# Transposing the second batch's keys and queries with the DMA crossbar instead of TensorE, in memory lent by weights that are not yet loaded

## The chip, the cores and the metric

The kernel runs on one core of a Trainium2 chip. The metric is device time in microseconds (us) of one execution. Times below are medians. A span given by a profile is 1 to 2 us shorter than the time of an execution.

## The reference, cut to what matters

```python
# 4 batches, 8 heads, 768 tokens, 64 dimensions, 16 clusters per head
q_assign = argmax(einsum('bhsd,hcd->bhsc', q_n, c_n)); k_assign = ...      # fp32 decides the cluster
mask   = q_assign[:, :, :, None] == k_assign[:, :, None, :]
attn   = softmax(where(mask, q @ k.T / 8, -1e9)) @ v
x      = attn as (3072, 512)
out    = sum over 4 experts e of p[:, e] * (relu(x @ w1[e]) @ w2[e])       # 512 -> 1024 -> 512
```

Every key and query is needed transposed (dimension on the partitions), in fp32 for the cluster scores and in bf16 for attention.

## The kernel before

TensorE works through attention steps and expert matmuls woven together. A generator per batch ("preparation") is paced beside them: so many of its steps between two attention steps. For batch 1 it transposes on TensorE. Batches 2 and 3 already go over the DMA crossbar (the transposing path of the DMA engines), which the program gives 16-bit elements: each fp32 tensor is **split** by GpSimd into low and high halves, the halves are **crossed** (transposed) by DMA, and GpSimd **merges** them again.

```python
class Assign:
    def turn(self, y, copy, shared=False):          # one head, three 128x128 fp32 transposes on TensorE
        ...
        nc.tensor.matmul(tp[:, c0:c0 + 128], raw[...][:, ...], ident, is_transpose=True)
        ...
        copy(t32, tp[:, :m * w])                    # PSUM to SBUF, VectorE in batch 1
    def cast(self, y, r, copy): ...                 # fp32 to the bf16 rows of KF or QF, GpSimd in batch 1
    def scores(self, copy): ...                     # four fp32 matmuls (TensorE), one copy
    def back(self): ...  # transposes the scores;  top(): marks the best cluster with a one-hot row (VectorE)
    def send(self, j, r):                           # one-hots to 16 rows of KF or QF
        (nc.gpsimd if self.b or ... else nc.sync).dma_start(...)

class Crossed(Assign):
    def split(self, n): ...                         # pool(h16[...], raw[...][:, z::2]), 768 halves a partition
    def cross(self, j): ...                         # nc.sync.dma_start(out=t16, in_=h16, transpose=True)
    def merge(self, n): ...                         # pool(all[...][:, z::2], t16[...])
    def casts(self): ...                            # two VectorE casts of 64x1536

def load_w(e):                                      # 2 x 2 MB fp32 from HBM, cast to bf16 by the DMA
    nc.gpsimd.dma_start(out=W1[e], in_=...)
    nc.gpsimd.dma_start(out=W2[e], in_=...)

for y, x in enumerate(xs):                          # keys 0-3, queries 0-3, keys 4-7, queries 4-7
    if b == 1:                                      # preparation of batch 1, 31 steps
        t = 12 * (y // 2) + 4 * z
        for j in range(HG):
            put(t + j, lambda x=x, j=j: turn(x, j)) # turn on TensorE, two casts on GpSimd
        ...
        put(at, lambda x=x: x.scores(dve))
        put(at + 1 + z, x.back, x.top, x.scale_onehot, x.cross_onehot)
        put(at + 4 + z, x.send_all)
...
put(1 + 18 * g, lambda g=g: load_w(2 + g))          # experts 2 and 3
```

Each engine has one queue, which in all traces here it works off in program order; SyncE's queue issues the crossings, GpSimd's the weight loads and the sends.

The softmax here doesn't subtract the row's maximum and nothing guards it: scores larger than these inputs give would overflow.

## Time and profile before

| | before |
|---|---|
| time, median of 4 runs | 475.19 us (475.13 to 475.93) |
| TensorE busy | 98% of the span |
| VectorE, ScalarE, GpSimd busy | 48%, 58%, 39% |
| granted TensorE clock | 1.000 |
| first matmul of expert 2 / of expert 3 | 85.28 us / 101.32 us |

The last row gives two landmarks: TensorE's first 128x128 matmul group of expert 2 and of expert 3. All preparation of batch 1 that concerns us lies before the second. The lines of the page are shown in the prediction.

### The profile page before, as it was taken

How to read it: one execution, taken by the hardware profiler on the slowest of the kernel's cores; microseconds unless marked ns; L12 is line 12 of the kernel's file. 1: busy time of each engine (PE TensorE's matmuls, PEld its weight loads, DVE VectorE, ACT ScalarE, POOL GpSimd, SP SyncE). 2: the span in 40 equal slices, each digit the busy share in tenths (PEclk: the TensorE clock that was granted, in tenths of full speed). 3: DMA queues.
4: the chain of work that ended last, by engine and by line, in shares of the span. 5: the costliest groups of instructions: out<-in, count | busy, mean ns of one | idle time of the engine just before them, and what ended most of it. 6: DMA issues, size and time to landing. Idle time of an engine off the chain costs nothing.

```text
span 474.3 us, 11380 instructions
## 1 busy us (share of the span) xinstructions
PE 466.8 (98%) x4529; PEld 331.6 (70%) x4529; DVE 226.0 (48%) x558; ACT 277.1 (58%) x502; POOL 186.1 (39%) x301
## 2 busy tenths in 40 slices
PE   8999999999999999999999999999999999999997
PEld 4778777776776767677676767776766766667665
DVE  5964764321316664321234544423878767675112
ACT  5757655445665656566565655665665675664442
POOL 5936469180653694450442933000332132220000
PEclk9999999999999999999999999999999999999999
DMA  8999962927664940603657545202100100100101
GB/s 278 259 211 344 241 128 42 177 44 174 96 122 114 199 118 18 159 15 62 150 141 123 115 114 160 68 16 73 50 13 8 54 10 8 36 28 12 44 2 44
DMA packets 75981, 48.27 MB, mean 102 GB/s; under 512 B 51544, under 2 KB 70680, under 8 KB 75928
## 3 DMA queue, kind: packets, MB, share of 16 engines
q1 hardware_dynamic: 66680, 38.22, 32.7%
q0 software_dynamic: 8576, 9.25, 11.0%
q8 instruction: 35, 0.57, 0.6%
q10 hardware_dynamic: 672, 0.08, 0.1%
q14 instruction: 18, 0.15, 0.1%
HBM read 37.31 MB, written 6.30 MB: 92 GB/s over the span
## 4 chain that ended last, share of the span: by engine, by line
PE 94%; DVE 2%; DMA 2%; SPq 0%; issue 0%; ACT 0%; ACTq 0%
PE ps_mo L724 35%; PE ps_mo L743 35%; PE ps_s L634 9%; PE ps_av L661 7%; PE ps_s L547 1%; DMA raw<-in_q_dram 1%; DMA kf<-oht 1%; PE ps_misc L242 1%; PE ps_misc L547 1%; PE ps_misc L400 1%; PE ps_mo L400 1%; PE ps_mo L242 1%; DVE kf L315 1%; PE ps_mo L267 0%; PE ps_misc L267 0%; DVE oh L287 0%
## 5 line engine op out<-in xcount | busy, mean ns | idle before, releaser
L640 ACT ACTIVATE at<-ps_s 128x512 bf16<-128x512 f32 x252 | 147.7, 596 | 119.0 <-PE ps_s L634 103.9
L724 PE MATMUL ps_mo<-xT,w1b 128*128 128x256 bf16 (+1 forms) x1664 | 195.8, 264 | 0.0
L743 PE MATMUL ps_mo<-w2b,hT 128*128 128x512 bf16 (+2 forms) x784 | 190.3, 375 | 0.0
L724 PEld LDWEIGHTS <-w1b 128*128 128x128 bf16 x1664 | 146.3, 98 | 25.1 <-issue 1.2
L730 ACT ACTIVATE hT<-ps_mo 128x512 bf16<-128x512 f32 x192 | 114.7, 598 | 60.7 <-PE ps_mo L724 58.0
L752 DVE SCALAR_TENSOR_TENSOR oacc<-ps_mo,psb,oacc 128x512 f32<-128x512 f32 (+1 forms) x74 | 54.3, 734 | 130.7 <-PE ps_mo L743 130.4
L743 PEld LDWEIGHTS <-hT 128*128 128x128 bf16 x784 | 67.1, 98 | 57.5 <-issue 3.1
L634 PE MATMUL ps_s<-qf,kf 80*128 80x256 bf16 (+1 forms) x456 | 82.5, 267 | 0.9 <-ACT at L640 0.4
L661 PEld LDWEIGHTS <-at 128*128 128x128 bf16 x1152 | 69.9, 97 | 15.3 <-issue 1.7
L661 PE MATMUL ps_av<-vx,at 128*128 128x65 bf16 x1152 | 80.3, 193 | 0.0
L647 POOL TENSOR_TENSOR at<-at,same 128x512 bf16<-128x512 bf16 x24 | 28.2, 1174 | 98.5 <-ACT at L640 82.8
L634 PEld LDWEIGHTS <-kf 80*128 80x128 bf16 x456 | 42.0, 98 | 20.8 <-issue 1.9
L564 DVE TENSOR_SCALAR same<-qf,late 128x256 bf16<-128x256 bf16 x144 | 39.3, 324 | 0.0
L377 POOL COPY t<-t 128x768 uint16<-128x768 uint16 x32 | 35.5, 1116 | 0.0
L647 DVE TENSOR_TENSOR at<-at,same 128x512 bf16<-128x512 bf16 x48 | 21.6, 449 | 25.7 <-ACT at L640 25.7
L358 POOL COPY h<-raw 128x768 uint16<-128x768 uint16 x16 | 13.0, 825 | 37.3 <-DMA raw<-in_q_dram 30.7
L668 DVE RECIPROCAL zr<-ps_av 128x4 f32<-128x4 f32 (+1 forms) x50 | 8.9, 178 | 33.9 <-PE ps_av L661 33.8
L361 POOL COPY h<-raw 128x768 uint16<-128x768 uint16 x16 | 13.0, 826 | 28.9 <-DMA raw<-in_q_dram 20.4
L336 POOL DMA_DIRECT2D kf<-oht x32 | 15.4, 496 | 22.8 <-DMA oht<-oh 13.1
L750 DVE TENSOR_SCALAR oacc<-ps_mo,psb 128x512 f32<-128x512 f32 x18 | 13.5, 749 | 22.7 <-PE ps_mo L743 22.7
L416 POOL COPY st<-sct 128x384 uint16<-128x384 uint16 x16 | 10.6, 708 | 31.7 <-DMA sct<-scs 31.7
L336 POOL DMA_DIRECT2D qf<-oht x40 | 20.0, 509 | 6.2 <-DVE oht L313 3.9
(130 smaller groups left out, 281.5 us busy)
## 6 DMA issues: line engine op xcount, KB each, us to landing
raw<-in_v_dram SPq DMA_DIRECT2D x8, 768.0 KB, 5.7
out_dram<-oacc SPq DMA_DIRECT2D x23, 256.0 KB, 2.2
raw<-in_k_dram SPq DMA_DIRECT2D x7, 768.0 KB, 6.3
raw<-in_q_dram SPq DMA_DIRECT2D x6, 768.0 KB, 5.3
w1b<-in_moe_w_dram POOLq DMA_DIRECT2D x4, 1024.0 KB, 11.5
w2b<-in_moe_w_dram POOLq DMA_DIRECT2D x4, 1024.0 KB, 16.8
qf<-nos SPq DMA_DIRECT2D x2, 768.0 KB, 4.0
xT<-xn SPq DMA_TRANSPOSE x80, 2.4
```

The lines of the kernel that those rows point to most:

```text
L336: (nc.gpsimd if self.b or self.i0 and self.g else nc.sync).dma_start(out=self.rows(slice(D, D + CL), j, r), in_=self.oht[p0:p0 + CL, :self.w])
L377: pool(self.all[:, y * w:(y + 1) * w].bitcast(U16)[:, z::2], self.t16[:, (2 * z + y) * w:(2 * z + y + 1) * w])
L564: nc.vector.tensor_scalar(same[:, x * 256:(x + 1) * 256], clusters(b)[:, g, w, k // 2, k % 2, :], key_nos[b % 2][:, g, 8 * i + 4 * (k // 2 ...
L634: nc.tensor.matmul(sp[:, x * n:(x + 1) * n], KF[b % 2][:K, h, r, i * 128:(i + 1) * 128], QF[b % 2][:K, h, rs[0]:rs[-1] + 1, w * 128:(w + 1 ...
L640: nc.scalar.activation(at, sp, ACT.Exp, scale=scale)
L647: (nc.gpsimd if n4 in POOL_STEPS else nc.vector).tensor_tensor(at, at, same_cluster(b, w, cur), op=ALU.mult)
L661: nc.tensor.matmul(av[:, h % 2, m, :], at[:, c0:c0 + 128], VX[b % 2][:, h, 2 * i + r, :], start=(first and x == 0 and m == 0), stop=(last ...
L724: nc.tensor.matmul(ph[:, x * n:(x + 1) * n], W1[e][:, i, (f + x) * 128:(f + x + 1) * 128], xT[:, i, :], start=(i == 0), stop=(i == ND - 1))
L730: nc.scalar.activation(ht, ph, ACT.Relu)
L743: nc.tensor.matmul(po, hT[f // per][:, c0:c0 + 128], W2[e][:, f, c], start=(f == 0), stop=(f == NF - 1))
L750: nc.vector.tensor_scalar_mul(oacc, po, pap)
L752: nc.vector.scalar_tensor_tensor(oacc[:, c], po, pap, oacc[:, c], op0=ALU.mult, op1=ALU.add)
```

## The change

The intent is to take 48 fp32 transposes off the engine that bounds the kernel, TensorE, and with them their copies out of PSUM (TensorE's output memory) off VectorE. Memory for the halves is short; the change puts those of the first two tensors into the weight buffers of experts 2 and 3, so those weights can be loaded only later. The core of the diff:

```diff
+        def lent(self, w):
+            return w[self.borrows].rearrange("p i c -> p (i c)").bitcast(U16)[:, :2 * HG * QW]
...
+        if b == 1:
+            xs[0].borrows, xs[1].borrows = 2, 3
             for y, x in enumerate(xs):
+                g, z = divmod(y, 2)
+                t, late_cross = 16 * g + 4 * z, 3 * (y == 3)
                 for j in range(HG):
-                    put(t + j, lambda x=x, j=j: turn(x, j))
+                    put(t + j, lambda x=x, j=j: x.split(j))
+                    put(t + 1 + j + late_cross, lambda x=x, j=j: x.cross(j))
+                    put(t + 8 + j + (late_cross > 0), lambda x=x, j=j: x.merge(j))
+                put(t + 12 + (late_cross > 0), x.take_all, x.casts)
+                put(16 * g + 18, lambda x=x: x.scores(dve))
+                put(16 * g + 19 + z, x.back, x.top, x.scale_onehot, x.cross_onehot)
+                put(16 * g + 23 + z, x.send_all)
+            put(0, lambda: load_raw(upto=11))
+            put(13, lambda: load_w(2))
+            put(25, lambda: cast_v(b, 0), lambda: load_w(3))
+            put(28, lambda: load_raw(2, upto=13))
+            put(36, lambda: cast_v(b, 1))
...
-    XSTEPS = [0, 31, 63, 63]
+    XSTEPS = [0, 41, 63, 63]
```

More of the change, by code (lines that the diff above doesn't have):

```diff
@@ L344, with take_all @@
     class Crossed(Assign):
+        borrows = None
         def halves(self, x):
             return x.rearrange("p j c -> p (j c)").bitcast(U16)
+        def lent(self, w):
+            return w[self.borrows].rearrange("p i c -> p (i c)").bitcast(U16)[:, :2 * HG * QW]
+        def take_all(self):
+            self.t32s = [self.all[:, j * QW:(j + 1) * QW] for j in range(HG)]
         def split(self, n):
@@ L353, in split @@
             if n == 0:
-                self.h16 = self.halves(raws.tile([128, HG, QW], F32, name="h16", tag="raw"))
+                self.h16 = (self.lent(W1) if self.borrows is not None else
+                            self.halves(raws.tile([128, HG, QW], F32, name="h16", tag="raw")))
             dst = self.h16.rearrange("p (s y a j d) -> p s y a j d", s=2, a=A, j=2, d=D)
@@ L365, in cross @@
             if j == 0:
-                self.t16 = self.halves(raws.tile([128, HG, QW], F32, name="t16", tag="raw"))
+                self.t16 = (self.lent(W2) if self.borrows is not None else
+                            self.halves(raws.tile([128, HG, QW], F32, name="t16", tag="raw")))
             c = slice(j * 2 * QW, (j + 1) * 2 * QW)
@@ L466, in put @@
             todo.setdefault(at, []).extend(fs)
-        def turn(x, j):
-            x.turn(j, dve)
-            for r in range(2):
-                x.cast(j, r, pool)
-        for y, x in enumerate(xs):
-            z = y % 2
-            if b == 1:
-                t = 12 * (y // 2) + 4 * z
-                for j in range(HG):
-                    put(t + j, lambda x=x, j=j: turn(x, j))
-                put(t + 3, lambda: load_raw(upto=13))
-                at = 12 * (y // 2) + 8
-            else:
-                t = 8 * y
+        if b == 1:
+            xs[0].borrows, xs[1].borrows = 2, 3
+            for y, x in enumerate(xs):
+                g, z = divmod(y, 2)
+                t, late_cross = 16 * g + 4 * z, 3 * (y == 3)
@@ L483, in assigns @@
                 for j in range(HG):
                     put(t + j, lambda x=x, j=j: x.split(j))
-                    put(t + 2 + j, lambda x=x, j=j: x.cross(j))
-                    put(t + 9 + j, lambda x=x, j=j: x.merge(j))
-                put(t + 6, load_raw)
-                put(t + 15 + 4 * z, x.casts)
-                at = 16 * (y // 2) + 24
-            if b == 1:
-                put(at, lambda x=x: x.scores(dve))
-                put(at + 1 + z, x.back, x.top, x.scale_onehot, x.cross_onehot)
-                put(at + 4 + z, x.send_all)
-                continue
+                    put(t + 1 + j + late_cross, lambda x=x, j=j: x.cross(j))
@@ L495, in assigns @@
+            put(36, lambda: cast_v(b, 1))
+        for y, x in enumerate(xs if b > 1 else ()):
+            z = y % 2
+            t = 8 * y
+            for j in range(HG):
+                put(t + j, lambda x=x, j=j: x.split(j))
+                put(t + 2 + j, lambda x=x, j=j: x.cross(j))
+                put(t + 9 + j, lambda x=x, j=j: x.merge(j))
+            put(t + 6, load_raw)
+            put(t + 15 + 4 * z, x.casts)
+            at = 16 * (y // 2) + 24
             put(at, lambda x=x, t=("mo", "misc")[z]: x.scores_split(t))
@@ L504, in assigns @@
             put(at + 14 + 6 * z, x.spread_numbers)
-        for g in range(2):
-            if b == 1:
-                put(1 + 18 * g, lambda g=g: load_w(2 + g))
-                put(26 + 3 * g, lambda g=g: cast_v(b, g), lambda: load_raw(upto=13))
-            else:
-                for j in range(HG):
-                    put(36 + 8 * g + j, lambda g=g, j=j: cast_v(b, g, (j,)))
-                put(40 + 8 * g, load_raw)
+        for g in range(2 if b > 1 else 0):
+            for j in range(HG):
+                put(36 + 8 * g + j, lambda g=g, j=j: cast_v(b, g, (j,)))
+            put(40 + 8 * g, load_raw)
         for at in range(XSTEPS[b]):
@@ L893 @@
         gens.append(Paced(assigns(b), XSTEPS[b], PER_B * (b - 1) if b > 1 else S1 + 7,
-                          PER_B * b - (2 if b > 1 else -2)))
+                          PER_B * b - (2 if b > 1 else -6)))
     def woven(works, upto):
```

## The prediction

> **What bounds the kernel now.** I read the page's busy table first, then the chain that ended last, cut to the stretch in which the second batch is prepared, then the engines in order of time there. All times are microseconds.
>
> ```profile
> PE 466.8 (98%) x4529; PEld 331.6 (70%) x4529; DVE 226.0 (48%) x558; ACT 277.1 (58%) x502; POOL 186.1 (39%) x301
> PE   8999999999999999999999999999999999999997
> POOL 5936469180653694450442933000332132220000
> PEclk9999999999999999999999999999999999999999
> ```
>
> TensorE is busy from end to end at full clock: work taken from its queue shortens the program one for one, and any wait put into its in-order queue lengthens it one for one. GpSimd is at 39% on average, but slices 4 to 8 (35 to 95 us) hold 4, 6, 9, 1, 8: its room lies in waits, and this is where the change puts its work.
>
> The change concerns the 16 groups of three fp32 transposes of batch 1, found in the chain (start, duration, what) from 41.5 to 67.2. Samples:
>
> ```profile
> 41.54 0.36 PE ps_misc L242 x3
> ...
> 46.24 0.36 PE ps_misc L242 x3
> ...
> 59.76 0.49 PE ps_misc L242 x3
> ...
> 66.88 0.36 PE ps_mo L242 x3
> ```
>
> The eight groups of heads 0 to 3 sum to 2.9 us on the chain, the eight of heads 4 to 7 to 3.0: **5.9 us**, 1.2% of the program. (The 273 ns median of one such matmul is pipelined latency, not what it costs the chain, which is 0.12.)
>
> The cost of what replaces them is seen where batches 2 and 3 already go that way, in the groups by form:
>
> ```profile
> L377 POOL COPY t<-t 128x768 uint16<-128x768 uint16 x32 | 35.5, 1116 | 0.0
> L361 POOL COPY h<-raw 128x768 uint16<-128x768 uint16 x16 | 13.0, 826 | 28.9 <-DMA raw<-in_q_dram 20.4 <-DMA raw<-in_k_dram 8.4
> L336 POOL DMA_DIRECT2D kf<-oht x32 | 15.4, 496 | 22.8 <-DMA oht<-oh 13.1 <-DMA w2b<-in_moe_w_dram 5.5 <-DMA w1b<-in_moe_w_dram 4.2
> L258 POOL CAST kf<-t 64x384 bf16<-64x384 f32 x30 | 15.3, 511 | 4.1 <-ACT t L252 1.6 <-DVE t L252 1.4
> L387 DVE CAST kf<-t 64x1536 bf16<-64x1536 f32 x4 | 4.5, 1118 | 1.6 <-POOL t L377 1.6
> ```
>
> Each row has busy time, mean ns of one, idle before. Back to back on GpSimd a split starts every 0.77 (102.33 to 105.46 for four) and an undisturbed split-merge pair takes 1.73, so a merge 0.96.
>
> GpSimd's order of time around the last weights (start, duration):
>
> ```profile
> 79.57 0.81 POOL L153 DMA_DIRECT2D w1b<-in_moe_w_dram  x1
> 80.38 0.92 POOL L154 DMA_DIRECT2D w2b<-in_moe_w_dram  x1
> 81.26 2.95 POOL L336 DMA_DIRECT2D kf<-oht  x6
> 88.40 0.49 POOL L336 DMA_DIRECT2D kf<-oht  x1 [4.19 <-DMA w1b<-in_moe_w_dram]
> 94.35 0.49 POOL L336 DMA_DIRECT2D kf<-oht  x1 [5.47 <-DMA w2b<-in_moe_w_dram]
> ```
>
> After the two weight loads six sends go out, the seventh waits for the first load to land, the eighth for the second: here no more than eight transfers of this queue are outstanding. Before the change that costs nothing, since only batch 1's attention, steps later, needs what GpSimd makes.
>
> **What the Trainium skill says.** "VectorE: DVE Perf Modes", section The three transpose paths, gives 390 ns for a 128x128 bf16 transpose on TensorE (into PSUM) and 1309 ns on the crossbar (into SBUF). The crossbar is the slower way to the result but leaves TensorE free; here one transfer of six blocks lands in a median 2.8 us and occupies the SyncE queue 1.25. "DMA: Bandwidth & Descriptors", section DMA Transpose (X-bar), allows 2-byte types only: hence the halves, and the splits and merges. The same page, section SWDGE vs HWDGE vs iDMA, says that the queues of GpSimd and SyncE feed different internal queues of the same DMA engines, served in turn. The trace agrees that they share: a crossbar transfer of xT lands in a median 2.4, but in 5.4 while weights load (80 to 95). "SBUF — State Buffer", in its first section, says that one of VectorE and GpSimd blocks while the other holds the shared port pair, for instance in a fast VectorE cast. The trace agrees: the merge at 150.60 took 1.77 instead of 1.04 beside the two L387 casts at 149.01.
>
> **The change part by part.**
> Removed: 48 transposes on TensorE, -5.9 on the chain; 16 evacuations on VectorE (16 x 0.555 = 8.9) and 32 casts on GpSimd (32 x 0.51 = 16.4), both beside other work.
> Added: on GpSimd 16 splits (16 x 0.77 = 12.3) and 16 merges (16 x 0.96 = 15.4), net +11.3; on VectorE 8 casts of 64x1536 (8 x 1.1 = 8.8), net nothing; 16 crossbar transfers on SyncE (16 x 1.25 = 20 of queue time), a queue with room.
> Moved: the load of expert 2's weights from preparation step 1 to 13, expert 3's to 25; heads 0 to 3's scores from 8 to 18, the others' from 20 to 34. The generator's 41 steps run from attention step 35 to 78 (31 to 74 before).
>
> The dependency is what matters. Before, TensorE made the transposes itself and GpSimd's casts were a side product. After, TensorE's scores and VectorE's casts need GpSimd's merges, so GpSimd's in-order queue enters the chain. I lay both queues side by side.
>
> GpSimd comes free at 42.1 (its sends of batch 0 end). To the last merge that the second scores need it must do: 16 splits 12.3, 16 merges 15.4, two weight loads 2 x 1.73, 16 sends (two groups of 3.8) 7.6, four V casts 1.8: 40.6 in all. Thus **82.7 at the earliest**, without one wait.
>
> TensorE without waits: preparation step 34 is attention step 35 + 34 x 43/41 = 70.7, just after expert 2 begins at step 70. In the trace expert 2 begins at 85.3, and the steps after it take 2.7 each, so step 70.7 is at 87. Less 5.9 removed, less 2.1 for the second group's scores and turns that now come later: **79**. So even a GpSimd that never waits is 3.7 late.
>
> It will wait. (a) Heads 0 to 3: the raw queries land near 46.8 (issue 33.6, landing 13.2), so the second four splits end near 50, eight merges with the weight issue between them (1.7) near 59.4. TensorE reaches the first scores at about 56.4 and the second tensor's at 57.2: some 2.2 of wait, and VectorE then does the casts (2.2) before it copies the scores, which costs about 1.3 more: **3.5**. (b) The first sends need the one-hots, whose crossbar transfer leaves near 64 and lands near 69.5, as it runs against the weights issued at 56 (5.4 rather than 2.8). From there: sends to 73.4, the last split 74, sends 78, two merges 80, V casts and weights 83.5, six merges 89, with 0.8 lost to VectorE's casts: near 89 to 90. TensorE, now 3.5 later, arrives at 82.5: **7** of wait.
> Sum: -5.9 + 3.5 + 7 = +4.6. If GpSimd's waits vanish, only the 3.7 and part of (a) remain: about -1.
>
> **Rivals.**
> 1. The waits are hidden and the 5.9 is gained: 469.3. For it: the page's average of GpSimd, the same method working in batches 2 and 3, and a schedule that looks tuned (late crossings for the last tensor, loads after the lent memory is read). Against it: 40.6 of work in the 36.9 between 42.1 and 79. I have taken all durations from other stretches; if the pace of the steps is 4 us off, it holds.
> 2. Weights or DMA become the bound: expert 2's weights are issued near 57, land within 16 (75.9 to 94.4 is 14 for the next), needed from 80; expert 3's issued near 83, landed near 98, needed after 100. The trace before is against this by several us; it would cost 0 to 3.
> 3. VectorE, stuck in order at the casts behind the merges, fails to empty the PSUM banks of the experts, and TensorE stops earlier than at the scores. Three banks rotate there, so I find about 9 us of slack at the second casts; if this slack is smaller, the loss grows to 10 or 12 and the time to 484 or more.
>
> **Range and chances.** The gain is bounded by 5.9, so 469 is the floor and faster by over 2% (below 465.7) has hardly a chance. The working gives 479.8. Because the pace could be off in my disfavour I shade it to 478. The low end of 470 is rival 1 nearly whole; the high end of 486 is rival 3. Over 484.7 (slower by 2%) I give 0.12.
>
> **What would show it.** L242 in the chain of batch 1 gone, with about 5.9 less TensorE time: the first step. TensorE idle in front of L267 (the scores), its releaser a GpSimd merge L377 or a VectorE copy behind it, 2 to 4 us near 57 and 4 to 10 near 80: the main claim. GpSimd at 9 in slices 4 to 8; its sends L336 waiting on oht near 65 to 70. I am wrong if TensorE's row shows no gap between 50 and 95 (then 469 to 470), or if the gaps stand at expert matmuls L724 that wait for weights (rival 2) or for VectorE (rival 3).

## The result, and the profile after

| | before | after |
|---|---|---|
| time, median of 4 runs | 475.19 us | 491.79 us (490.79 to 492.25) |
| ratio | | 1.0343 (1.0329 to 1.0358): slower |
| granted TensorE clock, mean | 1.000 | 0.983 |
| first matmul of expert 2 / 3 | 85.28 / 101.32 | 83.06 / 117.82 |

Ratios are the mean time of one kernel's runs over that of the other's in the same rounds, so they are not quite the ratio of the medians. The result is correct. The prediction of 478 with a range of 470 to 486 failed: the time lies 16.6 us above the kernel before.

The page of the kernel after (busy share in 40 slices of 12.25 us, and the granted clock in tenths):

```profile
PE 465.8 (95%) x4430; PEld 328.2 (67%) x4481; DVE 232.0 (47%) x550; ACT 277.0 (57%) x502; POOL 203.1 (41%) x301
PE   7999889489999999999999999999999999999997
POOL 5928666966245469345055365100122223121000
PEclk9999999669999999999999999999999999999999
```

TensorE's row has one hole, in the eighth slice (86 to 98 us), with low clock there and in the next. Everything from slice 10 on is as before. In TensorE's own order of time (start, duration, what, and in brackets how long it stood idle just before and for whom), the hole reads:

```profile
83.06 0.61 PE L732 MATMUL ps_mo<-xT,w1b 128*128 128x128 bf16 x8
...
88.72 1.49 PE L267 MATMUL ps_misc<-t,bdc 128*32 128x384 f32 x4 [2.51 <-POOL t L387]
94.14 1.50 PE L267 MATMUL ps_misc<-t,bdc 128*32 128x384 f32 x4 [3.92 <-POOL t L387]
96.04 1.50 PE L267 MATMUL ps_mo<-t,bdc 128*32 128x384 f32 x4 [0.41 <-POOL t L387]
99.46 1.49 PE L267 MATMUL ps_mo<-t,bdc 128*32 128x384 f32 x4 [1.93 <-POOL t L387]
...
117.82 0.61 PE L732 MATMUL ps_mo<-xT,w1b 128*128 128x128 bf16 x8
```

Here L267 computes the scores of heads 4 to 7, and its releaser is each time a GpSimd merge, L387: the releaser that the prediction named (it has the line numbers of the kernel before, where the merge is L377 and the expert matmuls are L724 and L743; after, they are L387, L732 and L751). How much is lost where follows from the landmarks. Without any wait expert 2 would begin at 85.3 - 5.9 (transposes gone) - 2.1 (scores moved behind it) = 77.3 and expert 3 at 101.3 - 5.9 = 95.4. They begin at 83.1 and 117.8. So **5.8 us are lost before expert 2 (heads 0 to 3) and 16.6 more before expert 3 (heads 4 to 7)**; 5.8 + 16.6 - 5.9 = 16.5, which is the measured loss.

TensorE's two longest waits for heads 0 to 3 look different. They are not at L267 and not for GpSimd, but for VectorE, whose cast (third line) had itself waited for merges and so held up what stood behind it:

```profile
58.35 0.29 PE L685 MATMUL ps_mo<-identb,xn 128*128 128x128 bf16 x2 [2.16 <-DVE xn L678]
66.33 0.55 PE L276 MATMUL ps_misc<-ident,scs 128*128 128x128 f32 x3 [1.80 <-DVE scs L271]
```
```profile
55.04 2.71 DVE L397 CAST kf<-t 64x1536 bf16<-64x1536 f32 x2 [2.56 <-POOL t L387]
```

Why the merges come so late is in the chain of waits, from 71 us on (start, duration, what):

```profile
71.58 6.05 DMA oht<-oh
...
78.24 3.17 POOL kf L336 x7
...
82.93 2.26 POOL qf L336 x5
...
86.67 1.99 POOL t L387 x2
88.66 1.76 POOL vx L149 x4
90.42 0.76 POOL w1b L153
91.18 0.91 POOL w2b L154
92.09 2.53 POOL t L387 x3
94.62 0.29 issue
94.91 4.50 POOL t L387 x3
```

The one-hot of heads 0 to 3 (oht) leaves only at 71.6 and needs 6 us; behind it stand sixteen sends (L336), one split, two merges, the V casts (L149), the issue of expert 3's weights (L153, L154) and six more merges, all in one queue. And the start of it, on SyncE's queue and on VectorE:

```profile
43.41 14.34 SPq L378 DMA_TRANSPOSE w2b<-w1b  x8
67.31 4.17 SPq L694 DMA_TRANSPOSE xT<-xn  x2
71.58 2.05 SPq L430 DMA_TRANSPOSE oht<-oh  x1
```
```profile
94.11 4.40 DVE L397 CAST kf<-t 64x1536 bf16<-64x1536 f32 x2 [19.11 <-POOL t L387]
99.63 4.62 DVE L397 CAST qf<-t 64x1536 bf16<-64x1536 f32 x2
```

The first eight crossings (in lent memory, hence w2b<-w1b) take 1.79 on average instead of 1.25: three of them hold the queue for 2.3 to 2.7. Two transposes of xT (the attention output on its way to the experts) then hold it for 4.2, and the one-hot, which VectorE had ready at 69.0, leaves behind them. VectorE, at a cast, waited 19.1 for the merges; its two casts then take 4.4 where such pairs took 1.9 to 2.6 in the kernel before.

### The profile page after: what moved, and what is told of

The parts are those of the page before. It is cut to its first block, busy times and chain, and to the rows that moved or that the text cites. A ratio compares the mean times of both kernels' runs of the same rounds, so it can differ in the third digit from the quotient of the medians.

```text
span 490.1 us, 11262 instructions
## 1 busy us (share of the span) xinstructions
PE 465.8 (95%) x4430; PEld 328.2 (67%) x4481; DVE 232.0 (47%) x550; ACT 277.0 (57%) x502; POOL 203.1 (41%) x301
## 4 chain that ended last, share of the span: by engine, by line
PE 83%; POOL 6%; DMA 5%; DVE 3%; issue 2%; ACT 0%; SPq 0%; POOLq 0%; ACTq 0%
PE ps_mo L732 32%; PE ps_mo L751 31%; PE ps_s L642 7%; PE ps_av L669 6%; POOL t L387 3%; DMA w2b<-w1b 2%; POOL qf L336 1%; DMA oht<-oh 1%; PE ps_s L555 1%; DMA kf<-oht 1%; POOL kf L336 1%; PE ps_misc L555 1%; PE ps_s L87 1%; PE ps_mo L410 1%; DVE qf L397 1%
## 5 line engine op out<-in xcount | busy, mean ns | idle before, releaser
L732 PE MATMUL ps_mo<-xT,w1b 128*128 128x256 bf16 (+1 forms) x1664 | 196.5, 265 | 0.7 <-ACT hT L738 0.7
L751 PE MATMUL ps_mo<-w2b,hT 128*128 128x512 bf16 (+1 forms) x733 | 187.7, 377 | 2.5 <-issue 0.2
L732 PEld LDWEIGHTS <-w1b 128*128 128x128 bf16 x1664 | 146.2, 98 | 25.6 <-issue 2.2
L751 PEld LDWEIGHTS <-hT 128*128 128x128 bf16 x784 | 66.8, 98 | 59.4 <-issue 5.5
L655 POOL TENSOR_TENSOR at<-at,same 128x512 bf16<-128x512 bf16 x24 | 28.2, 1175 | 98.5 <-ACT at L648 83.0
L387 POOL COPY t<-t 128x768 uint16<-128x768 uint16 x40 | 44.8, 1145 | 0.0
L370 POOL COPY h<-raw 128x768 uint16<-128x768 uint16 x24 | 22.2, 939 | 29.5 <-DMA raw<-in_q_dram 19.4
L367 POOL COPY h<-raw 128x768 uint16<-128x768 uint16 x16 | 13.0, 827 | 37.4 <-DMA raw<-in_q_dram 30.9
L336 POOL DMA_DIRECT2D kf<-oht x32 | 15.4, 489 | 18.8 <-DMA oht<-oh 18.8
L336 POOL DMA_DIRECT2D qf<-oht x40 | 19.7, 500 | 8.3 <-DVE oht L313 3.9
## 6 DMA issues: line engine op xcount, KB each, us to landing
w2b<-in_moe_w_dram POOLq DMA_DIRECT2D x4, 1024.0 KB, 16.5
```

Of the source, the lines that this page charges most:

```text
L336: (nc.gpsimd if self.b or self.i0 and self.g else nc.sync).dma_start(out=self.rows(slice(D, D + CL), j, r), in_=self.oht[p0:p0 + CL, :self.w])
L370: pool(self.h16[:, z * HG * QW + c:z * HG * QW + c + 2 * QW], self.halves(raw[self.b, self.t, self.g])[:, 2 * c:2 * c + 4 * QW][:, z::2])
L387: pool(self.all[:, y * w:(y + 1) * w].bitcast(U16)[:, z::2], self.t16[:, (2 * z + y) * w:(2 * z + y + 1) * w])
L655: (nc.gpsimd if n4 in POOL_STEPS else nc.vector).tensor_tensor(at, at, same_cluster(b, w, cur), op=ALU.mult)
L732: nc.tensor.matmul(ph[:, x * n:(x + 1) * n], W1[e][:, i, (f + x) * 128:(f + x + 1) * 128], xT[:, i, :], start=(i == 0), stop=(i == ND - 1))
L751: nc.tensor.matmul(po, hT[f // per][:, c0:c0 + 128], W2[e][:, f, c], start=(f == 0), stop=(f == NF - 1))
```

## The experiments

Four theories, each of which could make the second group's merges late. **1:** order of GpSimd's queue, the sends in front of merges. **2:** DMA, the weight loads beside crossings and one-hots. **3:** VectorE, whose casts wait in its queue for merges, and where casts and GpSimd's copies block each other. **4:** the clock, which stays low after the hole. All edits are against the kernel after the change unless said otherwise.

| label | edit | us | ratio to before (interval) |
|---|---|---|---|
| after | | 491.8 | 1.034 (1.033, 1.036) |
| late_sends | first sends behind all merges | 491.6 | 1.035 (1.033, 1.036) |
| late_casts | VectorE's casts behind the one-hots | 487.8 | 1.026 (1.024, 1.027) |
| warm | matmuls in TensorE's waits | 493.9 | 1.038 (1.035, 1.041) |
| no_w2 | expert 2's weights not loaded | 484.6 | 1.020 (1.017, 1.022) |
| late_sends_w3 | late_sends, expert 3's weights later | 481.5 | 1.013 (1.011, 1.016) |
| reordered | all moves, more at once | 491.6 | 1.034 (1.033, 1.036) |
| g0_only | heads 0 to 3 alone | 480.4 | 1.011 (1.010, 1.013) |
| keys_only | keys alone, early weights | 503.3 | 1.059 (1.055, 1.064) |
| three_moves | late_sends_w3 and late_casts | 481.6 | 1.013 (1.010, 1.016) |
| g0_ordered | heads 0 to 3, reordered | 483.5 | 1.017 (1.015, 1.018) |
| g0_w2late | the same, expert 2's weights later | 483.2 | 1.016 (1.015, 1.018) |
| full_spaced | whole change, all findings | 477.4 | 1.004 (1.003, 1.006) |
| g0_spaced | heads 0 to 3, all findings | **473.4** | **0.996 (0.995, 0.997)** |

The kernel before measured 475.3 to 475.5 beside the runs from late_sends on. The result is correct in all of them but no_w2. The program that judges runs calls a difference under 2% "same", so all from late_sends_w3 on but reordered and keys_only count as that; the intervals say what is clear of noise.

### late_sends: only the order of the sends

```diff
-                put(16 * g + 23 + z, x.send_all)
+                put((34, 39)[g] + z, x.send_all)
```

> Only the 16 sends of the one-hots of heads 0 to 3 move on GpSimd, from preparation steps 23 and 24 to 34 and 35, behind all merges. Theory 1 (the sends, which wait 8.5 us for a one-hot and take 7.7, stand in GpSimd's queue in front of the last eight merges): those merges end near 88 instead of 99.4, TensorE's wait at the second scores falls from some 15 us to 3 to 5, and the time is 479 to 483. Theory 2 (the transfers are late because expert 2's weights are loaded beside them): the merges then wait for the crossings instead, and the time stays above 486.

Measured 491.6: nothing gained. The wait for the one-hot left GpSimd's queue as meant, and expert 3's weights were issued 10 us earlier (80.6 instead of 90.4). They fell upon the last crossings. From the chain of waits:

```profile
80.97 12.25 DMA t<-h
93.22 0.05 issue
93.28 1.99 POOL t L387 x2
```

A crossing that lands in 2.8 us undisturbed took 12.3 beside the load. Theory 1 alone falls as the explanation: the queue's order was one of two limits of nearly equal length, and lifting one gave the other's turn.

### late_casts: only VectorE's casts

```diff
-                put(t + 12 + (late_cross > 0), x.take_all, x.casts)
+                put(t + 12 + (late_cross > 0), x.take_all)
+                put(16 * g + 21 + z, x.casts)
```

> Only VectorE's eight casts of 64x1536 move, from just behind the merges to after the one-hots. Theory 3 (VectorE and GpSimd block each other: the casts take 2.2 a pair elsewhere and up to 4.6 here, seven splits take 7.1 instead of 5.4, six merges 7.3 instead of 5.8): splits and merges return to 0.77 and 0.96 us each, the first one-hot is ready 3 us sooner, and the time is 482 to 486. Theory 1 alone, with the lock a trifle: 489 to 491.

Measured 487.8, so 4.0 gained: between the two ranges expected, nearer to theory 3's. That casts and merges hinder each other is real: the same six merges, beside casts in the kernel after and without them here, from GpSimd's order of time:

```profile
92.06 7.34 POOL L387 COPY t<-t 128x768 uint16<-128x768 uint16 x6
```
```profile
91.15 5.82 POOL L387 COPY t<-t 128x768 uint16<-128x768 uint16 x6
```

But the one-hot still left only at 71.8 and the sends began at 77.3, after 9.7 of wait for it, so the casts are not why it is late. It was ready at 67.8 and stood on SyncE's queue behind the two xT transposes, which held that queue for 6.0 beside the load of expert 2's weights.

### warm: the low clock

```diff
         def scores(self, copy, fill=(0, 0)):
+                for _ in range(fill[j // 2] if j % 2 == 0 else 0):
+                    nc.tensor.matmul(sc[:, 384:], W1[0][:, 0, :128], W1[0][:, 0, :128], start=True, stop=True)
```

> Matmuls of 128 columns on weights, into a part of the scores' bank that nobody reads, are put before the second scores, sized to run about 8 us in the 14 that TensorE waits there. Theory 4 (of the loss, some 4 us is not waiting but TensorE at half clock after the wait, 88.7 to 106.3): granted clock stays near 1 and the time falls by 2 to 4, to 488 to 490. If the low clock does not matter, or the matmuls are not free, 491 to 495.

Stretches of TensorE's wait (start:end, length, then busy time and instruction count of TensorE, its weight loads, VectorE, ScalarE and GpSimd, then granted clock, DMA share, GB/s), first of the kernel after, then of warm (which puts 40, 75, 10 and 45 matmuls in front of the four halves of the second scores):

```profile
88.70:101.00 12.30, 6.03 (x17) 0.87 (x18) 6.82 (x7) 0.00 (x0) 12.30 (x14) 0.50 1.07 244
```
```profile
85.50:98.60 13.10, 12.38 (x186) 9.96 (x183) 5.28 (x2) 0.60 (x1) 13.10 (x16) 1.00 1.00 228
```

The matmuls ran in the wait and held the clock at 1.00, yet the time is 493.9, not lower. GpSimd is busy all of both stretches; its last merge ended 1.5 earlier than in the kernel after (97.9 against 99.4), the last of the added matmuls ran 0.8 past it, and behind the scores TensorE then waited 2.9 for VectorE. So a clock held up bought nothing here, and theory 4 falls as an explanation of the loss; what the low clock would cost with VectorE out of the way is not shown. That the clock halves after idling is what the Trainium skill says (TensorE: Matmul & The Clock Gate, section Why this matters for your kernels: no idle gaps over some 3 us). The trace agrees on the half, 0.50; the gap was shorter here, 2.5 us just before the clock fell at 88.6.

### no_w2: one weight load less (wrong result)

```diff
     def load_w(e):
+        if e == 2:
+            return
...  # expert 2's matmuls read W1[1], W2[1]
```

> The result is wrong on purpose: expert 2's weights are never loaded, its matmuls read expert 1's. Takes 4 MB of reads off the DMA engines between 59 and 76 us and 1.7 us off GpSimd. Theory 2 (this load delays the crossings and one-hots): the first one-hot lands in under 3 us instead of 6, GpSimd's sends start near 70 instead of 78.2, and the time falls by 6 to 9, to 483 to 486. Theory 1 with another cause of the late one-hot (VectorE late): falls by 2 to 3 only, to 489.

Measured 484.6, so 7.2 gained, as theory 2 expected. GpSimd's wait for the one-hot fell from 8.5 to 4.4 and its sends began at 72.6 instead of 78.2, first of the kernel after, then of no_w2:

```profile
78.24 3.86 POOL L336 DMA_DIRECT2D kf<-oht  x8 [8.53 <-DMA oht<-oh]
```
```profile
72.62 3.81 POOL L338 DMA_DIRECT2D kf<-oht  x8 [4.39 <-DMA oht<-oh]
```

By the landmarks the gain is all in heads 4 to 7: expert 2 began at 82.6 (0.4 earlier), expert 3 at 110.5 (7.4 earlier). Of the gain 1.7 can be the issue time that GpSimd saves. Together with late_sends this puts the DMA collision first. What remains above the kernel before, 9.3, is not this load.

The same pair of traces shows the collision directly. The first crossing of heads 4 to 7 landed 12.4 after its issue in the kernel after (63.51 to 75.90, when the load's second half landed, at 75.95) and 2.8 after it in no_w2. From 63.5 to 67.0 the kernel after moved 413 packets of the load and none of SyncE's queue; from 69 to 72 it moved 432 of the load and 425 of SyncE's, so a crossing went forward one packet for each of the load's. In no_w2 two crossings moved 1600 packets from 63 to 66. The load itself lost nothing in the kernel after: 16.1 to landing, and 15.9 in the kernel before.

### late_sends_w3, reordered, g0_only, keys_only

late_sends_w3 adds one line to late_sends:

```diff
-            put(25, lambda: cast_v(b, 0), lambda: load_w(3))
+            put(25, lambda: cast_v(b, 0))
+            put(33, lambda: load_w(3))
```

> late_sends with one more move: the load of expert 3's weights goes from preparation step 25 to 33, behind the last merge. In late_sends the last crossings landed 12.3 us after the first of the last three had been issued, beside that load. Theory 2 (each load of 4 MB that runs beside crossings delays them; freeing GpSimd's queue alone only exchanged one wait for the other): the last merge ends near 88 to 90 instead of 99, and the time is 479 to 483. If the crossings are late for another reason, 489 to 492.

Measured 481.5, as theory 2 expected. Two moves that together change no amount of work gained 10.3 where the first alone gained nothing. The last merge ended at 87.5 instead of 99.4.

reordered moved everything at once (expert 2's weights 13 to 16, scores 20 and 34, casts 24 to 38, sends 33 and 39, expert 3's weights 34):

> All moves at once, with the same work: expert 2's weights behind the merges of heads 0 to 3 (16), first scores at 20, VectorE's casts behind the one-hots, the first sends and expert 3's weights behind the last merges (33, 34), V casts at 28. If waits of order are all of the loss (theories 1, 2, 3 together): the second wait nearly vanishes, 472 to 478. If the amount of work in the stretch (DMA and GpSimd) is the bound: 478 to 484.

Measured 491.6: both expectations missed. Expert 2 began at 78.6, so the first group lost only some 1.3 (two steps of room before its scores, no cast in front of merges and no weight issue between them came together here). But expert 2's weights, issued at 60.8, again ran beside the second group's crossings, and GpSimd waited 10.0 for one of these; expert 3's weights, issued at 101.6, were then waited for (2.8 at its first matmul).

g0_only crosses heads 0 to 3 with the change's order and gives heads 4 to 7 back to TensorE:

> Only heads 0 to 3 go over the crossbar, with the change's order; heads 4 to 7 are transposed by TensorE as before. Keeps 2.9 us of the 5.9. My reading (the first group loses about 3.5 and the second nearly all the rest): 474.5 to 477. If the first group is what makes everything late (its merges, its late one-hots, the late weights): 480 or more.

Measured 480.4, in the second of the two ranges: my share of the first group was too small, 7.8 with the 2.9 that should have been gained. Waits of 0.5 to 0.9 add up there, five of them from 57 to 68 (4.0 in all), four of them for VectorE, and TensorE then ran at a mean clock of 0.86 until 80.

keys_only crosses half as much, but lends only expert 3's memory and loads expert 2's weights at step 6, just behind the first four splits on GpSimd's queue:

> Only keys go over the crossbar, queries by TensorE; only expert 3's memory is lent, so that expert 2's weights load early again (step 6), and the casts of keys come behind the one-hots. Half the crossings, GpSimd's added work halves. Keeps 2.9 of 5.9. If half the load fits the stretch: no wait of TensorE over 1 us, 472 to 474.5, ahead of both kernels. If even eight crossings delay the scores: 475 to 480.

Measured 503.3: both expectations missed, and the slowest of all, with half the crossings. It is the clearest view of theory 2. The same stretch of the kernel before, where these weights load beside a plain load, and of keys_only, where they load beside crossings (columns as above), and one piece of its chain of waits:

```profile
50.00:54.00 4.00, 4.00 (x47) 2.39 (x44) 2.52 (x6) 1.91 (x4) 3.53 (x8) 1.00 1.10 248
```
```profile
50.00:54.00 4.00, 4.00 (x65) 3.79 (x63) 2.57 (x7) 2.83 (x6) 0.00 (x0) 1.00 1.40 52
```
```profile
47.73 22.80 DMA w2b<-w1b
```

The DMA engines are called busy in both, but move 248 GB/s in the one and 52 in the other. The last line is one crossing that took 22.8 us. The weights suffered too: their second half landed after 27.1 instead of 15.9. Here a crossing and a weight load did worse than share the engines, both lost; in the kernel after only the crossings did. Why the rate falls, these runs do not show, nor what in the load matters (its cast, its packets or GpSimd's queue), since no run loads the weights in another way. Beside plain loads the rate holds, 314 to 367 GB/s from 43 to 48 us in the kernel after, but a crossing is late there too: the first landed after 7.2.

### three_moves, g0_ordered, g0_w2late

> late_sends_w3 with VectorE's casts moved behind the one-hots as in late_casts. In late_sends_w3 (481.5) TensorE's visible waits were 9 us, of which 7.7 for VectorE results that stood behind casts waiting for merges. Theory 3 (a cast that waits in VectorE's queue holds up what TensorE needs): 473 to 477. If the merges themselves are what TensorE would then wait for: 478 to 481.

Measured 481.6, no better than late_sends_w3 and above both ranges expected. The waits before expert 3 did shrink (it began at 102.9 instead of 105.8). But the first sends lie behind expert 3's weights in GpSimd's queue, as in late_sends_w3, and attention of batch 1 now waited longer for them (3.3, where it waited 0.8 there):

```profile
106.85 0.59 PE L644 MATMUL ps_s<-qf,kf 80*128 80x256 bf16 x2 [3.29 <-DMA qf<-oht]
```

g0_ordered crosses heads 0 to 3 only, with no weight load beside crossings and the casts behind the one-hots; g0_w2late moves expert 2's load from step 16 to 23.

> Only heads 0 to 3 over the crossbar (2.9 us kept), in an order that takes the findings in: no crossing beside a weight load (expert 2's at 16, after the crossings have landed; none later), VectorE's casts behind the one-hots, first sends at 27 and 28, expert 3's weights behind them. If crossings next to weight loads and casts in front of merges were what cost g0_only its 5 us: no wait over 1.5 in all, 472.5 to 474.5, ahead of the kernel before. If not: 476 to 480.

> g0_ordered with expert 2's weights at step 23 instead of 16, so that the first one-hots too land before the load. One-hots then land in under 3.5 us and the sends do not wait for them; but the weights land some 5 us later. If the weights are still in time: within 0.5 us of g0_ordered or better. If not: TensorE waits at expert 2's first matmuls and it is 2 to 5 us slower than g0_ordered.

Measured 483.5 and 483.2: g0_ordered a miss, and of my own making. Up to 57.3 us nothing was lost. Then I had set two of TensorE's transpose groups into one step, just behind VectorE's casts, with one PSUM bank for them:

```profile
69.58 0.90 PE L242 MATMUL ps_misc<-ident,raw 128*128 128x128 f32 x3 [4.32 <-DVE t L252]
```

TensorE waited 4.3 and ran the next five microseconds at half clock. g0_w2late lies within 0.5 of it, as expected, but tests nothing, since the two kernels do not differ in what they were to tell apart: GpSimd reached both loads at nearly the same time (60.7 and 60.1), since its queue had nothing to do between the two steps.

### g0_spaced and full_spaced: order against amount

The second diff is a summary in words.

```diff
 # g0_spaced, against g0_ordered
-                put(22 + z, x.casts)
+                put(25 + 3 * z, x.casts)
-                    put(24 + 2 * z + j // 2, lambda x=x, j=j: turn(x, j))
+                    put(26 + 4 * z + j, lambda x=x, j=j: turn(x, j))
-                put(28, lambda x=x: x.scores(dve))
+                put(34, lambda x=x: x.scores(dve))      # back 35, 36; sends 39, 40; V casts 38
```
```diff
 # full_spaced, against the kernel after
-        merges and casts in one step; scores 18, 34; first sends 23, 24 on GpSimd; load_w(3) at 25
+        casts 25, 26, 39, 40;         scores 21, 36; first sends 28 on SyncE;      load_w(3) at 33
```

> The whole change with all findings: scores at 21 and 36, casts behind the one-hots, expert 3's weights behind the last merge, the first 16 sends from SyncE's queue so that they do not lie behind those weights. Waits of order are gone; what is left is that sixteen crossings and two loads of 4 MB must pass the DMA engines between 43 and 96 us. If that amount is the bound: TensorE waits 4 to 8 us for expert 3's weights, 474 to 479. If not: 469 to 472.

> g0_ordered lost nothing up to the first matmul of unit 2 (57.3 us, 6.7 before that of the kernel before) and then waited 4.3 us for a VectorE copy behind two casts, because I had put two transposes groups into one preparation step, just behind the casts, and ran at half clock after it. Here the casts lie at 25 and 28 and the transposes of heads 4 to 7 one to a step from 26, scores at 34. If the crossings of heads 0 to 3 are now free: 472.5 to 474.5, faster than the kernel before. If the load of expert 3's weights, issued late, is what TensorE waits for: 475 to 479.

full_spaced measured 477.4: 14.4 of the 16.6 us that the change loses come back by order and by moving the first sixteen sends from GpSimd to SyncE. The two are not told apart here; late_sends_w3, with order alone, got 10.3 back. It is still 0.4% slower than the kernel before. Its chain from 87 us on begins with:

```profile
87.64 14.21 DMA w2b<-in_moe_w_dram
101.84 0.14 issue
101.98 0.38 PE ps_mo L751
```

In this order expert 3's weights are issued behind the last merge, so as not to hit the crossings, and so land after they are needed. Expert 3 began at 98.5 instead of the 95.4 of no wait, and waits for these weights (1.2) and for late xT transposes (1.7) follow. That sixteen crossings and two weight loads, kept apart, cannot fit between 43 us, when the keys are there, and the use of expert 3's weights, the limit by amount that rival 2 of the prediction was about, is not shown: expert 2's load still ran beside the first crossings of heads 4 to 7 (one landed after 11.6), and the DMA engines were busy only 0.60 from 58 to 63 and 0.61 from 75 to 87.

g0_spaced measured 473.4 and is faster than the kernel before by 0.4%, with an interval clear of 1, and than the kernel after. Half the crossings, over before expert 2's weights start, fit. TensorE's row of it, and its only wait over 0.3 between 40 and 140 us:

```profile
PE   8999999999999999999999999999999999999996
```
```profile
72.81 0.55 PE L242 MATMUL ps_misc<-ident,raw 128*128 128x128 f32 x3 [0.38 <-DVE t L252]
```

It keeps 2.1 of the 2.9 us that heads 0 to 3 offer.

## Why the prediction was wrong

**Right:** what bounds the kernel; the 5.9 us on the chain; that GpSimd's queue enters the chain and TensorE waits at the scores of L267 for merges (for heads 4 to 7; for heads 0 to 3 it waited for VectorE, as shown above); that the second group loses more than the first; that GpSimd waits for the one-hots; that the change is not faster by 2%.

**Wrong in size, the sum (predicted +4.6, shaded to +2.8; measured +16.6).** The terms:

- Part (a), heads 0 to 3: 3.5 predicted, 5.8 measured by the landmark. I let the last of the first eight merges end near 59.4; it ended at 62.7. The merges waited 4.2 in all for crossings, for which I had put in nothing: the eight took 1.79 on average on SyncE's queue, not the 1.25 of batches 2 and 3 that I had carried over, and the first landed after 7.2 beside the loads of queries.
- Part (b), heads 4 to 7: 7 predicted, 16.6 measured. This is the step that failed. It said that the one-hot "leaves near 64 and lands near 69.5"; it left at 71.6 and landed at 77.6. It left late because (a) was late, so that it was ready only at 69.0, and because two xT transposes, slowed by the load of expert 2's weights, stood before it on SyncE's queue until 71.5. The casts were not the reason (late_casts). From the sends on the prediction's 20 us of GpSimd work were 21.2.
- Under (b) lies one assumption. I took the price of a DMA collision from xT transposes beside weights in the kernel before, 5.4 instead of 2.4. But these were issued at 89.5 and 90.6, near the end of a load that landed at 94.1, and landed some 2 us behind it; the 5.4 was what was left of the load. A crossing issued early in a load waits for most of it: 12.4 in the change itself, 12.3 in late_sends, 22.8 in keys_only, and even the smaller xT transposes took 9.7 and 7.2 in the change. no_w2 shows that one such load costs 7.2 in the change itself, all of it in (b).

**Rival 1** (hidden waits) is refuted. **Rival 2** (weights or DMA as the bound, "0 to 3") was put too small and in the wrong form: weights were not late in the change itself; they made the crossings and one-hots late, and only when that was mended (reordered, full_spaced) were the weights themselves waited for. **Rival 3** (VectorE behind merges) is shown in part: casts behind merges cost 4.0 by late_casts, and VectorE stops TensorE for 2.2 and 1.8 in the first group. The stop at expert matmuls that it foresaw does not appear in the change itself; it appears in late_sends (1.6) and warm (2.9).

**Slips in its working.** The POOL digits 4, 6, 9, 1, 8 belong to 47 to 107 us; 35 to 95 has 6, 4, 6, 9, 1. Nor was GpSimd at 9 from there on after the change, as its signs said, but at 8, 6, 6, 6, 9: it waited more than it worked off. "75.9 to 94.4 is 14" should be 80.4 to 94.1, which is 13.7. The preparation before also begins at attention step 35; the 31 is its number of steps.

The loss was also not additive, as my sum made it: late_sends alone 0, with expert 3's weights 10.3; three_moves nothing over late_sends_w3. Each mended wait uncovered the next one, of nearly its length.

What stays open is why a crossing moves nothing in the first part of a weight load, how the two ruin each other's rate in keys_only, and whether a still better order exists for the whole change; full_spaced is one order, not a proof.

## What to carry to other kernels

Before handing a bound engine's work to a chain over other engines, add up what those engines' queues must do in that stretch, in order, and treat a transfer's landing time as valid only beside the neighbours, and at the moment of their course, with which it was measured. Keep crossbar transposes and large weight loads like these apart in time, and let no engine that serves the bound one stand in its queue at work that waits for the chain. If no order found lets the whole fit, try the half: here that half beats both kernels.

## What the Trainium skill lacked or had wrong

- "DMA: Bandwidth & Descriptors", section SWDGE vs HWDGE vs iDMA, has the engines serving the two kinds of queue in turn, and I read that as sharing. From 69 to 72 us of the kernel after it is so, packet for packet (432 and 425). No page has what this does to a crossing beside a casting load: 12.4 us instead of 2.8 in the change itself, none of its packets in the first 3.5 us; in keys_only 52 GB/s where the kernel before has 248, a crossing of 22.8, the load 27.1 instead of 15.9.
- "Advanced Engine Details and Errata", section X-Bar Transpose (TRN2), calls transpose DMAs as fast as regular ones, at 350 to 400 GB/s. Not so here: while a lone crossing moves its 128 x 768 x 2 bytes (197 KB), the engines are at 9 in the digits and the rate is 207 to 220 GB/s (before, 103 to 109 us; 302 at most with a second transpose beside it, after, 76 to 78 us), where plain loads ran at 314 to 367. With issue and landing it takes 2.8 us, 70 GB/s.
- No page has the limit seen on GpSimd's queue: with two weight loads and six sends outstanding the next send waited for the first load (before: 4.2 and 5.5 us; g0_only: 5.0 and 6.0). The runs do not tell whether it is the chip's or comes from how the program shares out its semaphores.
